# A decay buffer for each half, K's product on GpSimd alone, F's mask as one operation, and one order for all groups of chunks

## The chip, the cores and the metric

The kernel runs on one core of one Trainium2 chip. Its metric is the device time of one execution in microseconds (us), the median of several runs. The engines of the core work side by side, each through its own instructions in order: TensorE (PE, with weight loads as PEld), VectorE (DVE), ScalarE (ACT), GpSimd (POOL) and SyncE (SP), whose queue issues nearly all the DMAs. They wait for each other through semaphores.

## The reference, cut to what matters

A recurrence over 768 steps for 4 x 8 heads of dimension 40, and behind it a mixture of four attention experts.

```python
for t in range(768):                     # state is 40 x 40 for each batch and head
    y[t]  = r[t] @ state
    Sa    = state @ a[t]
    state = state * w[t][None, :] - outer(Sa, b[t]) + outer(v[t], k[t])
x = y, heads side by side                # (4, 768, 320)
...
for e in range(4):                       # causal attention, head dimension 64
    out += gate[e] * softmax(mask(x wq[e] (x wk[e])^T / 8)) (x wv[e]) wo[e]   # two experts of four per row
```

All is float32. The change lies in the recurrence alone.

## The kernel before, in words

**Chunks and groups.** The 768 steps are cut into `NC = 24` chunks of 32, and the chunks into `NW = 6` groups W of four. Within a chunk the recurrence is turned into products of matrices of 32 x 32 and 32 x 40, for all 32 heads. Sixteen heads lie in each half of the partitions (index s or t), and a group's heads and chunks are prepared in two halves, `a = 0` and `1`.

**Preparing a group.** `prep(W, a)` makes the operands of one half. Its pieces have one letter each, and "0" or "1" ahead of it in the schedules is the half:

- `w`, `e`: loads of the decays (EW) and of a (EA); `l`, `u`: loads of the keys' two partition halves (EK, into KB). Each goes through SP's queue.
- `a` (L179): a scan over the decays into SUF, their products to the chunk's end. `b` (L181, L182): a copy and a reciprocal for the next scan. `s` (L184): the scan into SC, their products from the chunk's start.
- `f`, `g` (L176): two range flags on ScalarE, which read EW and write into GB.
- `x` or `X` (L188): AB = EA * SC, two operations, on VectorE or GpSimd.
- `k`, `p`, `K`, `H` (L192): KB = KB * SUF, in place; `K` and `H` are the b part and the k part on GpSimd, two operations each, `p` is the b part on VectorE, `k` both parts on VectorE.

EW's second half lies in an area of KB for the first group, and all later groups use one buffer for both halves, so `1w` waits for the scans and flags of half 0.

**The inversion.** `m0` and `m1` (`mm`) make 64 products each (L208), masked into GB (L210) and transposed into GK (L211), which GpSimd masks twice (L213). `L` (L222) copies GB into MT, `t` with a number runs that many of the 28 steps (L230, L232) of a triangular inversion on VectorE, `T` (L234, L235) transposes the result, `B` and `D` (L241) spread it on ScalarE, and `P` and `Q` (L248, 128 products each) complete it; `Q` ends with an addition on VectorE (L255).

**A chunk.** `chunk(c)` has steps `v` (L293), `g` (L297, L299), `u` (L302, L304), `w` (L307, L308), `f` (L311 and the mask L314), `t` (L319, L320), `y` (L323, L325), `z` (L327 and the output's DMA), `q` (L334) and `s` (L343 and the state's update L350). `keys` (L279, L280) transposes the next chunk's keys. The mask is two operations on VectorE of 64 partitions by 512: `FX[q, t]` gets the half t of PF times a triangular mask; the blocks of FX off that half stay at the zeros that `fill` wrote.

**The order.** The loop over n runs the steps in the order of `MAIN`, ten slots (0 to 9) for each n, in which `f`, `t`, `y` and `z` belong to chunk n - 1, `v` to n + 1 and the rest to n. `SIDE` says what of the next group's preparation follows each slot: key r is the chunk relative to 4 (W - 1), and "/" goes to the next slot. `LOADS` adds the loads of the chunks' own operands. Each engine takes its instructions in this order. `START` prepares group 0, `AHEAD` loads and partly prepares group 1 before the loop, and `SIDE1` is an order of its own for the rest of group 1.

Of the kernel before, what the change touches and what calls it, by code (L numbers as in the profile page):

```python
# [7 lines left out]
F32 = mybir.dt.float32  # L8
AF = mybir.ActivationFunctionType
OP = mybir.AluOpType  # L10
# [11 lines left out]
NW, NC = 6, 24  # L22

SIDE = {
    -3: "/0w///0e",
    -2: "//////0l//0f0g/0a0b0s",
    -1: "1w0u0X0K0H/1a1b///1l/1e///1f1g1s1u1X",
    0: "1p1H///m0//////m1L",
    1: "/t14//B/////t14",
    2: "/T////////P",  # L30
    3: "///D//////Q",
}
START = "x0 0w 0l0u 0e 1w 1l1u 1e x1 c0 0a 0b 0f 0g 0k 0s 0x 1a 1b 1f 1g m0 1k 1s 1x x2 m1 L B k0 t28 T D"
AHEAD = "0w 0l0u 1l1u 0e 0a 0b 0f 0g 0s 0K 0H 0X 1w 1e"

SIDE1 = {
    0: "1a1b1K1H/1f1g/1s1X/m0",
    1: "////m1L/t4//t14",
    2: "/t10T//B",
    3: "///P///D///Q",  # L40
}


def layouts(r, k, v, w, a, b):
# [18 lines left out]

def constants():
    f = np.float32
    cm = np.zeros((128, 261), f)
    cm[:, :128] = np.eye(128)
    j = np.arange(128)
    cm[:, 128:160] = j[:, None] % 32 < np.arange(32)[None, :]
    cm[:, 160:192] = -(np.arange(32)[None, :] < j[:, None] % 32).astype(f)  # L70
    cm[:, 192] = -1.25
    cm[:, 193] = 0.8
    cm[:, 195] = j // 32 % 2 == 0
    cm[:, 196] = j // 32 % 2
    cm[:, 197:229] = cm[:, 128:160] * cm[:, 195:196]
    cm[:, 229:261] = cm[:, 128:160] * cm[:, 196:197]
    return {"CM": cm}


def recurrence(tc, ctx, I, xT, FL, CM, early, tail=None):  # L80
    nc = tc.nc
    ep = early.enter_context(tc.tile_pool(name="early", bufs=1, side="right"))
    sp = ctx.enter_context(tc.tile_pool(name="rec", bufs=1))
    pp = ctx.enter_context(tc.tile_pool(name="rps", bufs=1, space=PSUM))
    V, A, T, PL, SY = nc.vector, nc.scalar, nc.tensor, nc.gpsimd, nc.sync
# [7 lines left out]
    def ring(name, shape, n, pool=sp, dt=F32):  # L93
        return [pool.tile(shape, dt, name=f"{name}{i}") for i in range(n)]

    A.dma_start(CM, I["CM"])
    ident, mask, maskn, mask2 = CM[:, 0:128], CM[:, 128:160], CM[:, 160:192], (CM[:, 197:229], CM[:, 229:261])
    d1 = ep.tile([104, 1056], BF, name="D1")
    EW0 = ring("EW", [104, 1056], 1, ep)[0]
    SUFr = ring("SUF", [104, 1057], 2, ep)  # L100
    D1P = ring("D1P", [104, 1056], 1, ep)[0]
    MT = ring("MT", [128, 1056], 1, ep)[0]
# [22 lines left out]
    GT = ring("GT", [128, 8, 2, 40], 1)[0]  # L125
    XT = ring("XT", [104, 16, 64], 1)[0]
    EAr = EAr, GKr[1].rearrange("p n r t -> p (n r t)")[0:104, 0:1024].rearrange("p (n t) -> p n t", t=32)
    EWr = EW0, KBr[1].rearrange("p x c t n -> p (x c t n)")[0:104, 0:1056]

    D0 = SC128[2].rearrange("p n t -> p (n t)")[:, 0:2048].rearrange("p (n r t) -> p n r t", n=32, r=2)  # L130
    two = (0, 1)
# [4 lines left out]
    def fill(x):  # L136
        if x == 0:
            for t in EWr:
                V.memset(t[32:64], 1.0)
            PL.memset(KBr[0][32:64], 0.0)  # L140
            PL.memset(ABr[0], 0.0)
            V.memset(d1, 0.0)
            V.memset(d1[:, ::132], 1.0)
            for t in SUFr:
                V.memset(t[:, 1056:1057], 1.0)
            V.memset(FL, 0.0)
            V.memset(D1P, 0.0)
        elif x == 1:
            PL.memset(MT, 0.0)
            PL.memset(RB, 0.0)  # L150
            PL.memset(RX, 0.0)
            PL.memset(FX, 0.0)
            PL.memset(SD, 0.0)
            PL.memset(R2, 0.0)
        else:
            V.memset(PS[32:64], 0.0)
            V.memset(PF[32:64], 0.0)
            PL.memset(D0, 0.0)
            PL.memset(BD, 0.0)
            PL.memset(ABr[1], 0.0)  # L160
            PL.memset(KBr[1][32:64], 0.0)
# [3 lines left out]
    def prep(w, a):  # L165

        half = slice(32 * a, 32 * a + 32)
        EW, SUF, sc, ab, kb = EWr[a if w == 0 else 0], SUFr[a], SC[w % 3][:, half], ABr[w % 2][:, half], KBr[w % 2][:, 4 * a:4 * a + 4]
        pc, ea = PC[w % 3][:, 8 * a:8 * a + 8], EAr[a if w == 0 else 0]
        sv = SUF[:, 1:1057].rearrange("p (n c) -> p n c", c=33)  # L170
        def load(t, src, which=two):
            for s in which:
                SY.dma_start(t[rows(s)], I[src][w, a, s])
        def flag(x):
            i = 2 * w + a
            A.activation(GB[0:104].rearrange("p (h n) c -> p h n c", n=4), EW.rearrange("p (h n c) -> p h n c", n=4, c=33)[:, :, :, 1:33], AF.Relu, bias=CM[0:104, 192 + x:193 + x],  # L176
                         scale=1.0 - 2.0 * x, accum_out=FL[0:104, 2 * i + x:2 * i + x + 1])
        def suf():
            V.tensor_tensor_scan(SUF[:, 0:1056][:, ::-1], EW[:, ::-1], d1[:, ::-1], 1.0, op0=OP.mult, op1=OP.add)  # L179
        def per():  # L180
            V.tensor_copy(pc, sv[:, ::4, 0])  # L181
            V.reciprocal(D1P[:, ::132], pc)  # L182
        def pre():
            V.tensor_tensor_scan(flat(sc), EW, D1P, 0.0, op0=OP.mult, op1=OP.add)  # L184
        def amul(e):
            for s in two:
                x = ab[rows(s), :, 32 * s:32 * s + 32]
                e.tensor_tensor(x, ea[rows(s)], sc[rows(s), :, 0:32], op=OP.mult)  # L188
        def kmul(e, k):
            for t in two:  # L190
                x = kb[0:104, :, :, t, 32 * k:32 * k + 32]
                e.tensor_tensor(x, x, sv[:, :, 1:33].rearrange("p (x t c) n -> p x t c n", t=2, c=4)[:, :, t], op=OP.mult)  # L192
        return dict(w=lambda: load(EW, "EW"), e=lambda: load(flat(ea), "EA"),
                    l=lambda: load(kb.rearrange("p x c t n -> p (x c t n)"), "EK", (0,)),
                    u=lambda: load(kb.rearrange("p x c t n -> p (x c t n)"), "EK", (1,)),
                    f=lambda: flag(0), g=lambda: flag(1), a=suf, b=per, s=pre, x=lambda: amul(V), X=lambda: amul(PL),
                    k=lambda: (kmul(V, 0), kmul(V, 1)), p=lambda: kmul(V, 0), K=lambda: kmul(PL, 0), H=lambda: kmul(PL, 1))
# [84 lines left out]
    def chunk(c):  # L282
# [26 lines left out]
        def s_f():  # L309
            for x, t in heads:  # L310
                T.matmul(PF[rows(t, 64), 64 * x:64 * x + 64], VR[:, t, x], RB[:, :, x, t], start=True, stop=True)  # L311
            for t in two:
                q = rows(t, 64)
                V.tensor_tensor(FX[q, t], pf[q], mask[q, None, None, :].to_broadcast([64, 8, 2, 32]), op=OP.mult)  # L314
        def s_t():
            if c == 0:
                return
# [41 lines left out]
    def at(n, s, *fs):  # L359
        jobs.setdefault((n, s), []).extend(fs)  # L360

    def items(W, line, inv, td):

        fs, i = [], 0
        line = line.replace(" ", "")
        while i < len(line):
            x = line[i]
            if x in "LTPQBD":
                fs.append(inv[x])
                i += 1  # L370
            elif x == "t":
                j = i + 1
                while j < len(line) and line[j].isdigit():
                    j += 1
                m = int(line[i + 1:j])
                fs += td[:m]
                del td[:m]
                i = j
            else:
                y = line[i + 1]  # L380
                if x == "x":
                    fs.append(lambda y=y: fill(int(y)))
                elif x == "c":
                    fs += [lambda k=k, y=y: load_c(int(y), k) for k in (range(4) if y == '0' else (1,))]
                elif x == "m":
                    fs.append(lambda y=y: mm(W, int(y)))
                elif x == "k":
                    fs.append(lambda y=y: keys(int(y)))
                else:
                    fs.append(preps[W, int(x)][y])  # L390
                i += 2
        return fs

    preps = {(w, a): prep(w, a) for w in range(NW) for a in range(2)}
    for W in range(1, NW):
        inv = invert(W)
        td = list(inv["t"])
        for r, line in (SIDE if W > 1 else SIDE1).items():
            for k, part in enumerate(line.split("/")):
                n = 4 * (W - 1) + r  # L400
                assert k < 10
                at(max(n, 0), k if n >= 0 else 0, *items(W, part, inv, td))
        assert not td

    LOADS = {"v": lambda n: (n + 2, 0), "w": lambda n: (n + 1, 1), "y": lambda n: (n, 2), "f": lambda n: (n, 3)}
# [2 lines left out]
    for f in items(0, START, inv, list(inv["t"])):  # L408
        f()
    units[0]["v"]()  # L410
    for f in items(1, AHEAD, None, None) + items(0, "PQ", inv, None):
        f()
    load_c(1, 0)
    for n in range(NC + 1):
# [396 lines left out]
def body(tc, I, out):  # L811
    with ExitStack() as ctx:
# [24 lines left out]


_INS = {"EW": (6, 2, 2, 40, 1056), "EA": (6, 2, 2, 40, 1024), "EK": (6, 2, 2, 40, 2048), "V1": (24, 128, 320), "VX": (24, 2, 32, 640), "RB": (24, 2, 40, 512),
        "RX": (24, 2, 40, 512), "CM": (128, 261),  # L840
        "WQK": (128, 1536), "WVG": (128, 780), "WO": (128, 640), "MM": (128, 256), "RAW": (32, 768, 6, 40)}


# [18 lines left out]
```

## Time and profile before

| | before |
|---|---|
| median of 3 runs | 648.43 us (646.29 to 649.72) |
| the profiled execution | 647.44 us |
| its span, first to last instruction | 645.6 us |
| TensorE products, weight loads | 555.9 us (86%), 504.7 us (78%) |
| VectorE | 488.5 us (76%) |
| ScalarE | 347.3 us (54%) |
| GpSimd | 256.0 us (40%) |
| mean granted TensorE clock | 0.973 |
| L192 on GpSimd (KB) | 32 operations, 45.6 us |
| L188 on GpSimd (AB) | 20 operations, 44.5 us |
| L314 on VectorE (F's mask) | 48 operations, 32.8 us |

The recurrence takes the span up to about 385 us, the mixture the rest. A share of busy time is a mean over stages with different limits. In the chain that ended last each piece is the work that the next one waited for, so it says which engine set the time where. "issue" there is time in which an engine waited for nothing that the profile shows.

### The profile page before, as it was taken

The numbers are of one execution on the slowest core, as the hardware profiler recorded it, in microseconds if no ns is written. First come the engines' busy times: TensorE is split into PE (matmuls) and PEld (weight loads), VectorE is DVE, ScalarE is ACT, GpSimd is POOL, SyncE is SP. The second block draws the span as 40 slices with busy tenths as digits, with TensorE's granted clock in tenths as the row PEclk, the third lists the DMA queues.
The fourth block names the chain that finished last, engine by engine and source line by source line (L and its number), as shares of the span: only waits on it lengthen the run. The fifth ranks groups of instructions, "written<-read, shape, count | busy, mean of one in ns | idle before, by whom it ended". The sixth has DMA issues, their size and how long they took to land.

```text
span 645.6 us, 23340 instructions
## 1 busy us (share of the span) xinstructions
PE 555.9 (86%) x9961; PEld 504.7 (78%) x9961; DVE 488.5 (76%) x987; ACT 347.3 (54%) x726; POOL 256.0 (40%) x238
## 2 busy tenths in 40 slices
PE   0247689899899989989999987998999899999995
PEld 0237678889798988989899977887798787987784
DVE  7986487869769786886823346999998998798792
ACT  3015244545535634553544633775877686777883
POOL 7546812720651471075000023265353356234550
PEclk9999798999999999998999997998999999999998
DMA  5231124434523633452133625321312031110101
GB/s 169 64 103 35 54 82 126 105 91 120 153 67 96 154 80 116 107 151 66 49 88 81 188 58 128 97 50 57 87 46 78 6 86 58 55 27 23 62 2 67
DMA packets 42256, 53.82 MB, mean 83 GB/s; under 512 B 19808, under 2 KB 33376, under 8 KB 41184
## 3 DMA queue, kind: packets, MB, share of 16 engines
q1 hardware_dynamic: 42000, 52.12, 29.3%
q8 instruction: 80, 1.31, 0.9%
q14 instruction: 32, 0.26, 0.1%
q10 hardware_dynamic: 144, 0.13, 0.1%
HBM read 38.08 MB, written 7.86 MB: 71 GB/s over the span
## 4 chain that ended last, share of the span: by engine, by line
PE 54%; DVE 28%; issue 6%; ACT 4%; DMA 4%; SPq 0%; DVEq 0%; ACTq 0%
PE pk L248 6%; PE pt L619 5%; PE ot L744 4%; PE pf L323 4%; PE ps L343 3%; PE pk L208 3%; PE sc L699 3%; PE pt L755 3%; PE pf L325 3%; PE pt L729 3%; DVE TP L230 3%; DVE MT L232 3%; PE pg L293 3%; DVE m L709 3%; PE pk L279 3%
## 5 line engine op out<-in xcount | busy, mean ns | idle before, releaser
L721 POOL TENSOR_TENSOR P<-P,m 128x128 f32<-128x128 f32 (+2 forms) x96 | 89.1, 950 | 116.6 <-DVE m L717 61.4
L188 POOL TENSOR_TENSOR AB<-EA,SC 40x1024 f32<-40x1024 f32 x20 | 44.5, 2224 | 93.9 <-DVE SC L184 74.2
L710 ACT ACTIVATE P<-sc,m 128x128 f32<-128x128 f32 (+2 forms) x96 | 60.8, 634 | 26.0 <-DVE m L709 15.1
L744 PE MATMUL ot<-pt,vv 128*128 128x256 f32 (+1 forms) x384 | 61.1, 291 | 5.9 <-DVE ots L750 5.4
L699 PE MATMUL sc<-ks,qs 128*128 128x384 f32 (+4 forms) x256 | 62.7, 347 | 2.8 <-ACT P L710 1.9
L733 DVE TENSOR_TENSOR pt<-pt,pt 128x384 fp32r<-128x384 f32 (+1 forms) x96 | 59.0, 619 | 5.3 <-ACT pt L732 3.6
L709 DVE TENSOR_REDUCE m<-sc 128x1 f32<-128x128 f32 (+2 forms) x96 | 58.8, 616 | 1.1 <-PE sc L702 0.5
L744 PEld LDWEIGHTS ot<-pt,vv 128*128 128x128 f32 x384 | 51.3, 190 | 10.2 <-DVE ots L750 8.1
L732 ACT ACTIVATE pt<-pt 128x384 fp32r<-128x384 f32 (+1 forms) x96 | 52.0, 543 | 10.5 <-PE pt L729 9.0
L729 PE MATMUL pt<-CM,P 128*128 128x128 f32 x336 | 52.9, 275 | 3.9 <-DVE qs L628 2.6
L323 PE MATMUL pf<-FX,LS 128*40 128x64 f32 x768 | 47.7, 224 | 9.0 <-DVE FX L314 8.8
L192 POOL TENSOR_TENSOR KB<-KB,SUF 104x512 f32<-104x512 f32 x32 | 45.6, 1451 | 23.7 <-DVE SUF L179 12.4
L208 PE MATMUL pk<-KB,AB 104*64 104x64 f32 x768 | 29.6, 246 | 28.5 <-DVE AB L188 28.2
L323 PEld LDWEIGHTS pf<-FX,LS 128*40 128x40 f32 x768 | 42.3, 118 | 12.4 <-DVE FX L314 11.4
L314 DVE TENSOR_TENSOR FX<-pf,CM 64x512 f32<-64x512 f32 x48 | 32.8, 684 | 24.4 <-PE pf L311 24.0
L208 PEld LDWEIGHTS pk<-KB,AB 104*64 104x64 f32 x768 | 27.9, 159 | 29.6 <-issue 18.0
L619 PE MATMUL pt<-xh,wq 128*128 128x384 f32 x192 | 42.9, 359 | 4.4 <-DVE qs L628 4.2
L325 PE MATMUL pf<-RX,SD 80*40 80x64 f32 x736 | 45.9, 222 | 0.0
L699 PEld LDWEIGHTS sc<-ks,qs 128*128 128x128 f32 x256 | 40.7, 192 | 6.5 <-ACT P L710 5.9
L213 POOL TENSOR_TENSOR GK<-GK,CM 128x512 f32<-128x512 f32 x24 | 27.1, 1128 | 46.6 <-DVE GK L211 45.5
L299 ACT ACTIVATE GT<-pg,CM 128x320 f32<-128x320 f32 x48 | 22.7, 523 | 40.2 <-PE pg L297 40.2
L304 ACT ACTIVATE R<-pu 32x640 f32<-32x640 f32 x48 | 33.3, 693 | 19.4 <-PE pu L302 18.9
(147 smaller groups left out, 1388.1 us busy)
## 6 DMA issues: line engine op xcount, KB each, us to landing
KB<-in_EK SPq DMA_DIRECT2D x24, 320.0 KB
ks<-ks SPq DMA_DIRECT2D x32, 192.0 KB
V<-in_V SPq DMA_DIRECT2D x24, 160.0 KB
R<-in_VX SPq DMA_DIRECT2D x48, 80.0 KB
RX<-in_RX SPq DMA_DIRECT2D x48, 80.0 KB
RB<-in_RB SPq DMA_DIRECT2D x48, 80.0 KB
xT<-XT SPq DMA_DIRECT2D x24, 160.0 KB
out_dram<-o SPq DMA_DIRECT2D x24, 160.0 KB
```

The lines of the kernel that those rows point to most:

```text
L208: T.matmul(PK[rows(t, 64), x // 2, y:y + 64], ab[:, n], kb[0:104, 4 * a + x, c, t], start=True, stop=True)
L323: T.matmul(pf[rows(r), x], ls[:, x, r], FX[:, :, x, r], start=True, stop=c == 0)
L325: T.matmul(pf[rows(r), x], SD[:, x, r], RX[:, :, x, r], start=False, stop=True)
L619: T.matmul(p, w, x, start=(j == 0), stop=(j == len(prs) - 1))
L699: T.matmul(ps[:, c, 0:cw], QS[b][:, e, o], KS[b][:, e, z, k], start=(z == 0), stop=(z == 1 and not last), skip_group_check=True)
L709: V.tensor_reduce(m[:, 0, t:t + 1], ps[:, 0:ch, 0:cw], axis=AX.XY, op=OP.max, negate=True)
L710: later(DE, lambda: A.activation(pv, ps[:, 0:ch, 0:cw], AF.Exp, bias=m[:, 0, t:t + 1], accum_out=m[:, 1, t:t + 1]))
L721: PL.tensor_tensor(P[:, 0:n], P[:, 0:n], m[:, 3, t:t + 1].to_broadcast([128, n]), op=OP.mult)
L729: T.transpose(p[:, 128 * y:128 * y + 128], st["P"][t][:, 128 * c:128 * c + 128], ident)
L732: A.activation(h, p[:, 0:n], AF.Copy)
L733: later(DL, lambda: V.tensor_tensor(l, p[:, 0:n], f32(h), op=OP.subtract))
L744: T.matmul(po[:, 128:256] if one else po, VV[b][:, k, e].rearrange("p a b -> p (a b)"), PT[:, 256 * k:256 * k + (128 if one else 256)], st ...
```

## The change

- **EW has two buffers**, one for each half, in every group. The first group's second half no longer lies in KB.
- **K's product** of half 1 runs on GpSimd (`1K1H`), where half 0's did already; `p` is no longer used. It moves from slot 0 of the group's first chunk to slot 4 of the chunk before.
- **Loads** move: `0w` from slot 1 of r = -3 to slot 4 of r = -4, `1w` from slot 0 of r = -1 to slot 1 of r = -3, `0u` from slot 0 of r = -1 to slot 9 of r = -2, `1l` from slot 4 to slot 1, `1u` from slot 9 to slot 4 and `1e` from slot 5 to slot 6 of r = -1.
- **F's mask** is one operation over 128 partitions by 1024: PF is read twice along a broadcast axis and multiplied by a mask MK that is zero off the half. FX need not be cleared; MK comes with a second small load at the start.
- **Group 1** uses `SIDE` like the others. What `SIDE` puts before the loop stands in `AHEAD`, which now has both halves' scans and products, except `1f1g1s1X`, which follow slot 0 of the first chunk. `m1` and `L` of group 1 move from slot 4 of n = 1 to slot 9 of n = 0, and `P` from slot 3 of n = 3 to slot 9 of n = 2.
- The inversion's 28 steps are split 16 and 12 instead of 14 and 14.

```diff
--- before.py
+++ after.py
@@ -22,23 +22,18 @@
 NW, NC = 6, 24
 
 SIDE = {
-    -3: "/0w///0e",
-    -2: "//////0l//0f0g/0a0b0s",
-    -1: "1w0u0X0K0H/1a1b///1l/1e///1f1g1s1u1X",
-    0: "1p1H///m0//////m1L",
-    1: "/t14//B/////t14",
+    -4: "////0w",
+    -3: "/1w///0e",
+    -2: "//////0l//0f0g/0u0a0b0s",
+    -1: "0X0K0H/1l1a1b///1u1K1H//1e//1f1g1s1X",
+    0: "///m0//////m1L",
+    1: "/t16//B/////t12",
     2: "/T////////P",
     3: "///D//////Q",
 }
 START = "x0 0w 0l0u 0e 1w 1l1u 1e x1 c0 0a 0b 0f 0g 0k 0s 0x 1a 1b 1f 1g m0 1k 1s 1x x2 m1 L B k0 t28 T D"
-AHEAD = "0w 0l0u 1l1u 0e 0a 0b 0f 0g 0s 0K 0H 0X 1w 1e"
-
-SIDE1 = {
-    0: "1a1b1K1H/1f1g/1s1X/m0",
-    1: "////m1L/t4//t14",
-    2: "/t10T//B",
-    3: "///P///D///Q",
-}
+
+AHEAD = "0w1w 0l0u 1l1u 0e 0f0g 0a0b0s 0X0K0H 1a1b 1e 1K1H", "1f1g1s1X"
 
 
 def layouts(r, k, v, w, a, b):
@@ -63,7 +58,7 @@
 
 def constants():
     f = np.float32
-    cm = np.zeros((128, 261), f)
+    cm = np.zeros((128, 325), f)
     cm[:, :128] = np.eye(128)
     j = np.arange(128)
     cm[:, 128:160] = j[:, None] % 32 < np.arange(32)[None, :]
@@ -73,6 +68,8 @@
     cm[:, 195] = j // 32 % 2 == 0
     cm[:, 196] = j // 32 % 2
     cm[:, 197:229] = cm[:, 128:160] * cm[:, 195:196]
+    for t in range(2):
+        cm[:, 261 + 32 * t:293 + 32 * t] = cm[:, 128:160] * (j // 64 == t)[:, None]
     cm[:, 229:261] = cm[:, 128:160] * cm[:, 196:197]
     return {"CM": cm}
 
@@ -93,10 +90,12 @@
     def ring(name, shape, n, pool=sp, dt=F32):
         return [pool.tile(shape, dt, name=f"{name}{i}") for i in range(n)]
 
-    A.dma_start(CM, I["CM"])
+    MK = sp.tile([128, 64], F32, name="MK")
+    A.dma_start(CM, I["CM"][:, 0:261])
+    A.dma_start(MK, I["CM"][:, 261:325])
     ident, mask, maskn, mask2 = CM[:, 0:128], CM[:, 128:160], CM[:, 160:192], (CM[:, 197:229], CM[:, 229:261])
     d1 = ep.tile([104, 1056], BF, name="D1")
-    EW0 = ring("EW", [104, 1056], 1, ep)[0]
+    EWr = ring("EW", [104, 1056], 2, ep)
     SUFr = ring("SUF", [104, 1057], 2, ep)
     D1P = ring("D1P", [104, 1056], 1, ep)[0]
     MT = ring("MT", [128, 1056], 1, ep)[0]
@@ -125,7 +124,6 @@
     GT = ring("GT", [128, 8, 2, 40], 1)[0]
     XT = ring("XT", [104, 16, 64], 1)[0]
     EAr = EAr, GKr[1].rearrange("p n r t -> p (n r t)")[0:104, 0:1024].rearrange("p (n t) -> p n t", t=32)
-    EWr = EW0, KBr[1].rearrange("p x c t n -> p (x c t n)")[0:104, 0:1056]
 
     D0 = SC128[2].rearrange("p n t -> p (n t)")[:, 0:2048].rearrange("p (n r t) -> p n r t", n=32, r=2)
     two = (0, 1)
@@ -149,7 +147,6 @@
             PL.memset(MT, 0.0)
             PL.memset(RB, 0.0)
             PL.memset(RX, 0.0)
-            PL.memset(FX, 0.0)
             PL.memset(SD, 0.0)
             PL.memset(R2, 0.0)
         else:
@@ -165,7 +162,7 @@
     def prep(w, a):
 
         half = slice(32 * a, 32 * a + 32)
-        EW, SUF, sc, ab, kb = EWr[a if w == 0 else 0], SUFr[a], SC[w % 3][:, half], ABr[w % 2][:, half], KBr[w % 2][:, 4 * a:4 * a + 4]
+        EW, SUF, sc, ab, kb = EWr[a], SUFr[a], SC[w % 3][:, half], ABr[w % 2][:, half], KBr[w % 2][:, 4 * a:4 * a + 4]
         pc, ea = PC[w % 3][:, 8 * a:8 * a + 8], EAr[a if w == 0 else 0]
         sv = SUF[:, 1:1057].rearrange("p (n c) -> p n c", c=33)
         def load(t, src, which=two):
@@ -309,9 +306,8 @@
         def s_f():
             for x, t in heads:
                 T.matmul(PF[rows(t, 64), 64 * x:64 * x + 64], VR[:, t, x], RB[:, :, x, t], start=True, stop=True)
-            for t in two:
-                q = rows(t, 64)
-                V.tensor_tensor(FX[q, t], pf[q], mask[q, None, None, :].to_broadcast([64, 8, 2, 32]), op=OP.mult)
+            V.tensor_tensor(FX.rearrange("q t x s n -> q t (x s) n"), PF.rearrange("q (x n) -> q x n", n=32)[:, None].to_broadcast([128, 2, 16, 32]),
+                            MK.rearrange("q (t n) -> q t n", t=2)[:, :, None, :].to_broadcast([128, 2, 16, 32]), op=OP.mult)
         def s_t():
             if c == 0:
                 return
@@ -392,14 +388,15 @@
         return fs
 
     preps = {(w, a): prep(w, a) for w in range(NW) for a in range(2)}
+    at(0, 0, *items(1, AHEAD[1], None, None))
     for W in range(1, NW):
         inv = invert(W)
         td = list(inv["t"])
-        for r, line in (SIDE if W > 1 else SIDE1).items():
-            for k, part in enumerate(line.split("/")):
-                n = 4 * (W - 1) + r
+        for r, line in SIDE.items():
+            n = 4 * (W - 1) + r
+            for k, part in enumerate(line.split("/") if n >= 0 else ""):
                 assert k < 10
-                at(max(n, 0), k if n >= 0 else 0, *items(W, part, inv, td))
+                at(n, k, *items(W, part, inv, td))
         assert not td
 
     LOADS = {"v": lambda n: (n + 2, 0), "w": lambda n: (n + 1, 1), "y": lambda n: (n, 2), "f": lambda n: (n, 3)}
@@ -408,7 +405,7 @@
     for f in items(0, START, inv, list(inv["t"])):
         f()
     units[0]["v"]()
-    for f in items(1, AHEAD, None, None) + items(0, "PQ", inv, None):
+    for f in items(1, AHEAD[0], None, None) + items(0, "PQ", inv, None):
         f()
     load_c(1, 0)
     for n in range(NC + 1):
@@ -837,7 +834,7 @@
 
 
 _INS = {"EW": (6, 2, 2, 40, 1056), "EA": (6, 2, 2, 40, 1024), "EK": (6, 2, 2, 40, 2048), "V1": (24, 128, 320), "VX": (24, 2, 32, 640), "RB": (24, 2, 40, 512),
-        "RX": (24, 2, 40, 512), "CM": (128, 261),
+        "RX": (24, 2, 40, 512), "CM": (128, 325),
         "WQK": (128, 1536), "WVG": (128, 780), "WO": (128, 640), "MM": (128, 256), "RAW": (32, 768, 6, 40)}
```

## The prediction

> **What bounds the kernel now.** I read the page first (busy shares, the chain that ended last), then the windows by stage, then who waited for whom on TensorE, then the timeline around the long waits.
>
> ```profile
> PE 555.9 (86%) x9961; PEld 504.7 (78%) x9961; DVE 488.5 (76%) x987; ACT 347.3 (54%) x726; POOL 256.0 (40%) x238
> PE 54%; DVE 28%; issue 6%; ACT 4%; DMA 4%; SPq 0%; DVEq 0%; ACTq 0%
> ```
>
> TensorE carries most of the chain, VectorE a quarter. The change touches only the recurrence (0 to about 385 us); the mixture behind it is left alone. So I cut the recurrence at the starts of the key transposes (L279), one per chunk. Columns: window, its length, then busy us of each engine, granted clock, DMA share, GB/s.
>
> ```profile
> core 0: us, PE busy (x) PEld busy (x) DVE busy (x) ACT busy (x) POOL busy (x), PEclk, DMA share, GB/s
> 70.20:84.30 14.10, 12.42 (x281) 11.29 (x281) 3.59 (x6) 4.05 (x6) 8.49 (x6) 0.82 0.30 90
> 84.30:95.70 11.40, 9.98 (x256) 9.06 (x256) 10.57 (x31) 6.09 (x9) 2.55 (x4) 1.00 0.20 54
> 95.70:112.20 16.50, 15.27 (x387) 14.24 (x385) 12.81 (x14) 7.64 (x12) 4.32 (x2) 0.90 0.49 123
> 112.20:131.20 19.00, 17.25 (x451) 16.18 (x448) 15.13 (x15) 8.27 (x13) 13.80 (x10) 0.91 0.38 91
> 167.70:185.90 18.20, 15.80 (x449) 14.76 (x448) 15.73 (x15) 7.99 (x13) 12.85 (x9) 1.00 0.37 100
> 185.90:222.40 36.50, 35.28 (x964) 32.78 (x961) 27.68 (x50) 19.02 (x29) 8.86 (x8) 1.00 0.45 119
> 222.40:240.90 18.50, 16.40 (x451) 15.43 (x449) 15.78 (x15) 8.01 (x13) 13.95 (x10) 0.95 0.38 95
> 278.10:296.90 18.80, 16.99 (x451) 16.16 (x448) 15.24 (x15) 8.04 (x13) 13.08 (x9) 0.91 0.37 96
> 333.40:346.90 13.50, 13.50 (x387) 12.73 (x385) 4.41 (x6) 5.71 (x9) 0.00 (x0) 1.00 0.17 52
> 346.90:366.50 19.60, 19.60 (x516) 18.03 (x513) 5.78 (x8) 9.89 (x15) 0.00 (x0) 1.00 0.62 185
> ```
>
> The last two rows are the floor. A bare chunk is pure TensorE at 9.8 us (19.6 / 2). One with 128 inversion products (L248) is 13.5. An `mm` half adds 2.1 (L208, below). The stage at the head of a group holds one chunk, a set of L248 and an `mm` half: floor 15.6. It took 19.0, 18.2, 18.5 and 18.8. That is the largest loss, 12.1 us over four groups. The remaining three chunks (36.5, quoted once) have a floor of 9.8 + 9.8 + 13.5 + 2.1 = 35.2. The first group's three chunks took 14.1 + 11.4 + 16.5 = 42.0. Late chunks have nothing to win.
>
> ```profile
> PE pf L323 <- DVE FX L314: 8.8, 11, 2.1
> PE ps L319 <- issue: 1.8, 1, 1.8
> PE pu L302 <- issue: 1.7, 1, 1.7
> PE pk L248 <- issue: 1.7, 1, 1.7
> ```
>
> Those are TensorE's waits between 60 and 390 us. The three "issue" waits fall into the head stages of groups W=2, 3 and 5 (at 123, 175 and 288 us), and the longest L323 wait into that of W=4, so each head stage has one stop. In W=4 it is this:
>
> ```profile
> 232.89 3.85 DVE L192 TENSOR_TENSOR KB<-KB,SUF 104x512 f32<-104x512 f32 x2 [1.03 <-DMA KB<-in_EK]
> 233.91 2.08 PE L208 MATMUL pk<-KB,AB 104*64 104x64 f32 x64
> 236.66 1.38 DVE L314 TENSOR_TENSOR FX<-pf,CM 64x512 f32<-64x512 f32 x2
> 238.09 0.36 PE L323 MATMUL pf<-FX,LS 128*40 128x64 f32 x3 [2.10 <-DVE FX L314]
> ```
>
> VectorE waits for the second K load in `1p`, with the mask behind it, and TensorE waits for the mask.
>
> The three "issue" stops I read as TensorE's own instructions arriving late. The DMA queues ahead of the stop in W=5 (279.6 to 286.4 us), and at the same place of W=4 (224.3 to 231.3), in columns packets, MB and share of 16 engines:
>
> ```profile
> q1 hardware_dynamic: 380, 1.23, 71.1%
> ```
> ```profile
> q1 hardware_dynamic: 358, 1.21, 69.3%
> q8 instruction: 2, 0.03, 1.8%
> ```
>
> Same load on the data queue, but no instruction packet ahead of the stop and two where there was no stop. That is an inference from one pair. In W=2 the mask was late as well:
>
> ```profile
> 125.61 2.89 PE L208 MATMUL pk<-KB,AB 104*64 104x64 f32 x64
> 127.13 1.38 DVE L314 TENSOR_TENSOR FX<-pf,CM 64x512 f32<-64x512 f32 x2
> ```
>
> Without the 1.7 us stop TensorE would have been through with L208 at some 126.0, and the mask ended at 128.5. So there, and as I take it in W=3 and W=5, one of the two waits hides the other: removing the late mask alone gains almost nothing. After a stop the products are slower too: 64 of L208 took 2.89 here, 2.08 in W=4's row.
>
> **The change part by part.**
>
> *K on GpSimd alone, loads earlier.* Per group (W=2 to 5) two VectorE operations (3.85 us with their waits) leave the head stage, and GpSimd gets two more, 1.2 us each (median, next fence). SP issues the same loads, the last K load five slots earlier and its E load after it, with `0u` and `1w` out of the crowded chunk into the ones before. None waits for a reader there: every buffer it fills was read last at least a slot earlier. The mask then stands directly behind the inversion's add and is ready before TensorE asks. In W=4 that takes 18.5 to the floor plus 0.4 (the three-chunk stages stand 1.3 over theirs, some 0.4 a chunk), 16.0: **-2.5**. In the other three the gain is (19.0 + 18.2 + 18.8) / 3 - 16.0 = 2.7 each if the stop goes, near 0 if it stays. Of the large loads issued in the chunk ahead, an EW pair and one of three EK leave, about a third of the bytes, so I take one stop of three as gone: **-2.7** (bounds 0 and -8.1).
>
> GpSimd's queue in that chunk becomes 0X, 0K, 0H, 1K, 1H, 1X, then GK's masks. Its end, 1X, feeds the second `mm` half, one chunk later. Now, in W=3:
>
> ```profile
> 181.81 2.67 POOL L192 TENSOR_TENSOR KB<-KB,SUF 104x512 f32<-104x512 f32 x2
> 189.65 2.08 PE L208 MATMUL pk<-KB,AB 104*64 104x64 f32 x64
> ```
>
> GpSimd is done at 184.5 and the half starts at 189.7, so some 5 us cover the reordering.
>
> *F's mask in one operation.* Price of one by the nearest row of 1024 elements, half of 2.47:
>
> ```profile
> 15.25 2.47 DVE L188 TENSOR_TENSOR AB<-EA,SC 40x1024 f32<-40x1024 f32 x2
> ```
>
> So 1.23 instead of 1.38: 0.15 saved per chunk. Bounds: 1.38 (no gain) and 0.69, if one operation costs what one of the two costs now. It reaches the end only where TensorE waits for the mask: two chunks in each of four groups, 8 x 0.15 = **-1.2**. The dropped clear of FX and the second constant load lie in idle time at the start.
>
> *t16/t12 instead of t14/t14.* 28 steps between the same masks; state add and output come two steps later, some 0.5 us, while TensorE is busy with `v`. I take 0; if `v` did not cover it, +0.5 in each of five groups.
>
> *First group in the others' order, EW in two buffers.* Here everything is priced by these rows:
>
> ```profile
> 12.81 2.35 DVE L184 TENSOR_TENSOR_SCAN SC<-EW,D1P 104x1056 f32<-104x1056 f32 x1
> 52.16 6.66 POOL L192 TENSOR_TENSOR KB<-KB,SUF 104x512 f32<-104x512 f32 x4 [12.42 <-DVE SUF L179]
> 58.78 4.41 POOL L188 TENSOR_TENSOR AB<-EA,SC 40x1024 f32<-40x1024 f32 x2
> 61.50 3.91 DVE L179 TENSOR_TENSOR_SCAN SUF<-EW,D 104x1056 f32<-104x1056 f32 x1
> 63.25 2.09 PE L208 MATMUL pk<-KB,AB 104*64 104x64 f32 x64 [0.23 <-POOL AB L188]
> 68.85 0.66 DVE L210 TENSOR_TENSOR GB<-pk,CM 128x512 f32<-128x512 f32 x1
> 70.19 1.65 PE L279 MATMUL pk<-CM,KB 104*128 104x104 f32 x8 [4.85 <-DVE GK L211]
> 84.15 2.00 DVE L222 STREAM_TRANSPOSE MT<-GB 128x1024 f32<-128x1024 f32 x1
> 84.28 0.93 PE L279 MATMUL pk<-CM,KB 104*128 104x104 f32 x8 [1.49 <-DVE GK L211]
> 198.47 0.93 PE L279 MATMUL pk<-CM,KB 104*128 104x104 f32 x8
> ```
> ```profile
> L192 POOL TENSOR_TENSOR KB<-KB,SUF x32: 1170/1195/3235, 52.2 to 293.5; 104x512 f32<-104x512 f32 x32
> ```
>
> The scan at 61.50 took 3.91: it waited for GpSimd's product to end (58.78 + 4.41 = 63.19), then ran 2.36. So a scan and a GpSimd product take turns. The Trainium skill's "GPSIMD Engine Reference", section "Key points", says that GpSimd shares its SBUF interfaces with VectorE and contends with instructions that have two SBUF inputs. The trace agrees (3.91 against 2.35); the rule speaks against moving work to GpSimd, and the first rival below prices it.
>
> The new order starts 0X only behind `0s` (52.5 + 2.4 = 54.9), and 0K, 0H behind 0X. With scans `1a` and `1s` taking turns: 54.9 + 4.4 + 4 x 1.2 + 2 x 2.36 + 0.4 for the copies = 69.2 before `m0` can start; now 63.25. `m0`, cold, takes 2.1 to 3.7 (I take 3.3), mask and transpose 1.4: first L279 at 73.9, now 70.19, **+3.7**. The four TensorE steps up to `m1`, some 0.4 of a bare chunk or 3.9, reach it at 77.8; it waits for 1X, 69.2 + 4 x 1.2 + 4.4 = 78.4, and ends at 80.5. VectorE's mask, transpose (together 1.3) and MT (2.0) and F's mask (1.2) end at 85.0, then some 0.9 of L323: second L279 at 85.9, now 84.28, +1.6. From there the group runs like W=3, where 198.47 to 222.4 is 23.9: fourth L279 at 109.8, now 112.2: **-2.4** over all. The time is regained since `m1` no longer stands just ahead of L279 (1.49 there) and the inversion starts a chunk earlier. Bounds: 36.5 less the L325 and state transposes that chunk 0 lacks (an estimate: 0.9 each, like 8 L279) is 34.7 against 42.0, so -7.3; and +3.7 if nothing is regained.
>
> **Sum:** -2.5 - 2.7 - 1.2 - 2.4 = -8.8 us. The profiled execution (647.44 us; its span of 645.6 and 1.8 around it) goes to 638.6; against the median of 648.43, which lies 1.0 higher, 639.6.
>
> **The rivals.**
>
> *GpSimd becomes the wait (slower).* One queue now holds both K halves and 1X. If its products ran at 6.66 / 4 = 1.67 with VectorE taking turns, and the late K load still held 1K, 1X would end 4 x 0.5 + 2.4 later plus the load's delay. It decides when 1X ends after the time `mm` needs it, 189.7 in W=3 (187 with the stage shortened). At 4 us beyond that, each of four groups loses 4 - 2.7 = 1.3, and the first group adds 4 to its -2.4: 5.2 + 1.6 - 1.2 = +5.6, 654.0. For it: 69.2 and 78.4 above are already on the path. Against: 5 us of cover, and GpSimd busy only 13 of 18 us in the head stages.
>
> *The stops stay.* Then the mask's lateness was covered in three groups: -2.5 - 1.2 - 2.4 = -6.1, 642.3; with a new stop in W=4 and no net gain at the start, -1.2: 647.2, no change that can be told. For it: the count of instructions and of large loads is the same, only their spacing changes. The Trainium skill's "Runtime: NRT & Kernel Launch", section "Instruction fetch mechanics", says that fetching is mostly hidden behind slower dispatch. By that rule the three stops are something else and stay, which is this rival's time; the missing q8 row speaks against the rule, but only once.
>
> *All stops go:* -8.8 - 5.4 = -14.2, 634.2.
>
> **How the numbers follow.** Forecast (one stop of three goes, give or take 3 us at the start) 0.45; stops stay but the rest works, 0.15; all go, 0.12; stops stay and the start gives nothing, 0.17; GpSimd becomes the wait, 0.11. About 0.5% (3.2 us) is what a measurement of this kernel can tell from no change. The first three and little of the others end below 645.2: faster 0.71, same 0.17, slower 0.12. Range 633 to 648.5: from "all go" to the no-change case, leaving out the slower rival and a little at the bottom.
>
> **What would show it.** Right: no VectorE L192 after 40 us; L314 24 times at about 1.2; head stages at 16 to 16.5 unless they hold an "issue" wait; first L279 near 74, the fourth near 110. Wrong: L208 waiting for GpSimd in the groups from W=2 on; "issue" waits still in three or four head stages or moved to the chunk before; a scan held by GpSimd pushing the inversion's add past TensorE; or the mask at 1.4 or more.

## The result and the profile after

The changed kernel takes 632.7 us (median; 631.9 to 633.6) against 648.7 for the one before: ratio 0.976, interval 0.973 to 0.979. That is 7 us under the forecast of 639.6, a little under the low end of the range, and near the time of the rival "all stops go" (634.2). Measured again beside the kernel before, the same kernel stood at 0.978 (0.971 to 0.984) and 0.971 (0.967 to 0.974) of it. Executions over 1.5% above the fastest of their kernel are left out of the ratios, and the profiled ones of e1 and e2 are of that kind, so I read from them where a stop lies and not what the whole takes. In the changed kernel and those made from it the lines have other numbers: L276 for L279, L205 for L208, L208 for L211, L245 for L248, L309 for the mask (L314), L319 for L323, L189 for KB, L185 for AB, L181 for the scan into SC (L184), L299 for L302 and L315 for L319. In e2, e3 and e8, made from the kernel before, they are those of before. One slip in the text above: `1u` stood at slot 8 of the chunk before the group's first, not 9, so it moves four slots.

From the page of the changed kernel, busy shares, chain and two groups of instructions:

```profile
PE 550.8 (87%) x9961; PEld 500.5 (79%) x9961; DVE 476.1 (75%) x955; ACT 347.4 (55%) x726; POOL 276.8 (44%) x245
PE 60%; DVE 20%; issue 5%; ACT 4%; POOL 4%; DMA 4%; SPq 0%; DVEq 0%; ACTq 0%; POOLq 0%
L189 POOL TENSOR_TENSOR KB<-KB,SUF 104x512 f32<-104x512 f32 x40 | 66.3, 1690 | 0.6 <-DMA KB<-in_EK 0.2
L309 DVE TENSOR_TENSOR FX<-pf,MK 128x1024 f32<-128x1024 f32 x24 | 29.1, 1213 | 23.7 <-PE pf L308 23.7
```

VectorE's part of the chain falls from 28% to 20%; the shares of busy time hardly move. The stages, cut at the same places (columns as above):

```profile
73.50:86.80 13.30, 12.00 (x281) 11.00 (x281) 6.08 (x11) 4.79 (x8) 8.38 (x8) 0.84 0.20 58
86.80:97.80 11.00, 10.00 (x259) 9.07 (x257) 10.28 (x28) 5.35 (x8) 0.00 (x0) 1.00 0.35 101
97.80:111.30 13.50, 13.50 (x386) 12.73 (x385) 10.94 (x9) 8.19 (x13) 5.04 (x3) 1.00 0.54 150
111.30:126.90 15.60, 15.39 (x449) 14.63 (x448) 12.72 (x12) 8.00 (x13) 15.53 (x10) 1.00 0.34 88
162.80:179.40 16.60, 15.66 (x452) 14.75 (x449) 11.91 (x12) 8.03 (x13) 16.52 (x10) 1.00 0.29 84
179.40:215.20 35.80, 35.19 (x961) 32.72 (x960) 27.96 (x47) 18.99 (x29) 10.76 (x10) 1.00 0.48 132
215.20:230.60 15.40, 15.40 (x451) 14.62 (x448) 11.79 (x12) 8.05 (x13) 15.34 (x9) 1.00 0.33 90
266.50:281.90 15.40, 15.40 (x451) 14.63 (x449) 11.76 (x12) 8.01 (x13) 15.14 (x10) 1.00 0.33 89
```

Two head stages (W=4 and 5) are TensorE from end to end: 15.4 busy of 15.4. TensorE's waits between 60 and 390 us that answer to those above:

```profile
PE pk L205 <- POOL KB L189: 5.1, 2, 4.5
PE pf L319 <- DVE FX L309: 4.0, 6, 1.2
PE pk L245 <- issue: 0.9, 1, 0.9
```

One "issue" stop is left of three (0.9 us, W=3; a fourth one before, 0.7 us at L307, lay in the same stage and is gone too), and a wait for GpSimd is new, at the start. Where the 15.7 us of the recurrence went, by the starts of L276 against those of L279 (exact to 0.01):

| stretch | before | after | difference |
|---|---|---|---|
| start to the first key transposes | 70.19 | 73.47 | +3.3 |
| first to fourth (group 1) | 42.00 | 37.80 | -4.2 |
| the four head stages | 74.58 | 63.00 | -11.6 |
| all later chunks | 179.7 | 176.5 | -3.2 |
| up to the last key transposes | 366.48 | 350.82 | -15.7 |

Of the 3.2 us of the later chunks, 0.8 are one chunk of W=4 that before took 13.3 us at a granted clock of 0.93, where its like in the other groups took 12.5 to 12.6. What follows the last key transposes took 1.4 us more (645.6 - 366.5 = 279.1, now 631.3 - 350.8 = 280.5). Of these, 1.3 lie in the last stage of the recurrence, where the granted clock was 0.91 in this execution and 1.00 before.

### The profile page after: what moved, and what is told of

Read it like the earlier page. It is cut to its first block, busy times and chain, and to the rows that moved or that the text cites. A ratio compares the mean times of both kernels' runs of the same rounds, so it can differ in the third digit from the quotient of the medians.

```text
span 631.3 us, 23310 instructions
## 1 busy us (share of the span) xinstructions
PE 550.8 (87%) x9961; PEld 500.5 (79%) x9961; DVE 476.1 (75%) x955; ACT 347.4 (55%) x726; POOL 276.8 (44%) x245
## 3 DMA queue, kind: packets, MB, share of 16 engines
q8 instruction: 80, 1.31, 0.9%
## 4 chain that ended last, share of the span: by engine, by line
PE 60%; DVE 20%; issue 5%; ACT 4%; POOL 4%; DMA 4%; SPq 0%; DVEq 0%; ACTq 0%; POOLq 0%
PE pk L245 5%; PE pt L616 5%; PE ps L339 4%; PE ot L741 4%; PE pk L205 4%; PE pf L319 4%; PE sc L696 4%; PE pf L321 3%; PE pt L726 3%; PE pt L752 3%; PE pg L290 3%; PE pk L276 3%; DVE m L706 3%; PE pu L299 3%; PE pg L294 3%
## 5 line engine op out<-in xcount | busy, mean ns | idle before, releaser
L185 POOL TENSOR_TENSOR AB<-EA,SC 40x1024 f32<-40x1024 f32 x20 | 45.5, 2275 | 99.0 <-DVE SC L181 98.2
L189 POOL TENSOR_TENSOR KB<-KB,SUF 104x512 f32<-104x512 f32 x40 | 66.3, 1690 | 0.6 <-DMA KB<-in_EK 0.2
L205 PE MATMUL pk<-KB,AB 104*64 104x64 f32 x768 | 30.3, 247 | 33.7 <-DVE AB L185 28.5
L205 PEld LDWEIGHTS pk<-KB,AB 104*64 104x64 f32 x768 | 28.3, 160 | 34.9 <-issue 18.1
L319 PE MATMUL pf<-FX,LS 128*40 128x64 f32 x768 | 47.6, 224 | 4.3 <-DVE FX L309 4.0
L319 PEld LDWEIGHTS pf<-FX,LS 128*40 128x40 f32 x768 | 42.1, 118 | 7.5 <-DVE FX L309 6.4
L309 DVE TENSOR_TENSOR FX<-pf,MK 128x1024 f32<-128x1024 f32 x24 | 29.1, 1213 | 23.7 <-PE pf L308 23.7
L296 ACT ACTIVATE GT<-pg,CM 128x320 f32<-128x320 f32 x48 | 22.7, 523 | 42.2 <-PE pg L294 42.2
L726 PEld LDWEIGHTS pt<-CM,P 128*128 128x128 f32 x336 | 36.7, 141 | 7.4 <-issue 3.2
```

Source lines behind the costliest of these rows:

```text
L205: T.matmul(PK[rows(t, 64), x // 2, y:y + 64], ab[:, n], kb[0:104, 4 * a + x, c, t], start=True, stop=True)
L319: T.matmul(pf[rows(r), x], ls[:, x, r], FX[:, :, x, r], start=True, stop=c == 0)
L726: T.transpose(p[:, 128 * y:128 * y + 128], st["P"][t][:, 128 * c:128 * c + 128], ident)
```

## The experiments

They ask two things: what emptied the head stages, and what the start costs. Ratios are to the kernel before on the same chip. The kernel before spread from 643 to 657 us, the changed one over 1.7, 5.6 and 1.3 us on its three occasions, so single stages of a profile are often the sharper reading.

**e1: the mask alone.** Before, with MK and the single mask operation of the diff.

> The kernel before with F's mask as one operation and nothing else. Both theories: one operation at 1.21 us for two at 1.37 together, so 0.15 us where TensorE waits for the mask, at most 2 or 3 chunks of a group: 0.6 to 2 us less than before, head stages of the groups still at 18 to 19 us. If the mask alone were worth more (0.4 us in each of the chunks at the second and third place of a group, as the changed kernel has it), 3 us less.

Measured 0.998 (0.994 to 1.002): no difference that can be told. In its trace the second and third chunk of a group take 12.37 and 10.13 us (before 12.53 and 10.40), -0.43 a group. The head stages stay at 18.5 to 22.7.

**e2: K on GpSimd alone.**

```diff
-    0: "1p1H///m0//////m1L",
+    0: "1K1H///m0//////m1L",
```

> The kernel before with K's b part of half 1 on GpSimd instead of VectorE, at the same place in the order, loads as before. Theory 'crowd' (TensorE's instructions come late behind the crowd of loads): the 'issue' stops stay in three of the four head stages, which stay at 18 to 19 us; only the W=4 stage falls, to about 16: 2.5 us less in all. Theory 'mask' (VectorE's late mask is the loss and the stops only lie beside it): all four head stages fall to about 16: 10 to 12 us less.

Measured 0.992 (0.987 to 0.996). Head stages of W=2 to 5, and from TensorE's waits between 100 and 300 us those for the mask and the long stops:

```profile
111.10:128.00 16.90, 15.69 (x452) 14.74 (x449) 12.65 (x13) 8.27 (x13) 12.21 (x9) 1.00 0.45 110
164.40:188.20 23.80, 20.49 (x452) 19.10 (x449) 12.29 (x13) 8.05 (x13) 14.46 (x11) 0.78 0.29 76
224.60:240.00 15.40, 15.40 (x451) 14.63 (x448) 12.27 (x13) 8.05 (x13) 11.10 (x8) 1.00 0.43 115
276.50:297.40 20.90, 18.06 (x450) 17.08 (x449) 11.99 (x13) 7.98 (x13) 14.49 (x11) 0.84 0.35 87
```
```profile
PE pf L323 <- DVE FX L314: 3.6, 6, 0.7
PE pk L248 <- issue: 3.1, 1, 3.1
PE ps L319 <- issue: 2.8, 1, 2.8
PE pu L302 <- issue: 1.2, 1, 1.2
```

No long wait for the mask is left (0.7 at most), and W=4, which had only that, is at the floor. The three stops stay, in the same three stages and at the same lines. So far theory "crowd" has it right, though the three stages are at 16.9 to 23.8 us and not at 18 to 19, and the whole gained 5.4 us where it allowed 2.5.

**e3: the loads alone.** Before, with two EW buffers and the new slots of `w`, `u`, `l`, `e`; `1p1H` in its old place.

> The kernel before with two EW buffers and the new slots of the loads, K's product on VectorE in its old place, the mask as two operations, group 1 in its old order. Theory 'crowd': no 'issue' stop is left in the head stages, and K's load is there in time, so VectorE's product runs straight after the inversion's scan: head stages 16 to 16.5, 9 to 11 us less than before. Theory 'mask': the product still holds VectorE for 3.3 us in front of the mask, taking turns with GpSimd, and the head stages stay at 17.5 or more: 2 to 4 us less.

Measured 0.999 (0.995 to 1.003). The same views:

```profile
113.30:129.10 15.80, 15.73 (x453) 14.81 (x448) 12.09 (x12) 8.27 (x13) 11.53 (x8) 1.00 0.34 88
165.60:187.60 22.00, 18.87 (x451) 17.63 (x448) 15.63 (x15) 8.03 (x13) 14.21 (x9) 0.84 0.24 63
224.10:241.80 17.70, 15.63 (x449) 14.73 (x448) 16.76 (x15) 8.01 (x13) 14.49 (x9) 1.00 0.31 81
278.20:296.10 17.90, 15.83 (x453) 14.83 (x449) 16.92 (x15) 8.08 (x13) 14.69 (x9) 1.00 0.28 77
```
```profile
PE pf L323 <- DVE FX L314: 7.7, 8, 2.1
PE pk L248 <- issue: 2.8, 1, 2.8
```

Two of three stops are gone, but now the mask is late by some 2 us in W=4 and W=5, where VectorE's product still stands in front of it. Its load is there, but taking turns with GpSimd its two operations took 4.95 and 4.99 us in these stages; in W=2 they took 3.70, and the mask was in time. Neither theory gives both the stops and the times: there are two losses, and in W=5 e2 and e3 together show that each covers the other.

**e8: both, and nothing else of the change.** e3 with `1u1K1H` at slot 4 and no `1p1H`, so that K's product also starts earlier, as in the changed kernel.

> The kernel before with the loads' new slots, two EW buffers and K's product of half 1 on GpSimd at its new place, and nothing else: mask as two operations, 14 and 14 steps, group 1 in its old order. If the two waits hid each other, this pair gives what neither gives alone: head stages at 15.4 to 16, 9 to 12 us less than before, ratio 0.981 to 0.986. If parts simply add (0.9916 and 0.9992 alone), ratio 0.991.

Measured 0.979 (0.972 to 0.986). Alone the parts gave -0.8% and -0.1%, together -2.1%; -0.9%, the sum of the two, lies outside the interval. The changed kernel stands at 0.978 on the same chip, so these two parts are nearly all of the change. Its head stages (that W=3 has no stop in this execution may be chance, as the next runs show):

```profile
112.20:127.60 15.40, 15.40 (x452) 14.62 (x448) 10.88 (x12) 8.28 (x13) 15.25 (x11) 1.00 0.34 91
164.10:179.50 15.40, 15.40 (x452) 14.63 (x449) 12.03 (x13) 8.03 (x13) 14.89 (x9) 1.00 0.30 92
215.90:231.60 15.70, 15.50 (x453) 14.66 (x449) 12.93 (x13) 8.08 (x13) 15.62 (x10) 1.00 0.30 89
268.00:283.80 15.80, 15.61 (x454) 14.66 (x449) 12.07 (x13) 8.09 (x13) 15.04 (x10) 1.00 0.34 88
```

**e0 and e5: the changed kernel again, and the crowd put back.** e0 has no edit; this is e5's.

```diff
-    -3: "/1w///0e",
-    -2: "//////0l//0f0g/0u0a0b0s",
-    -1: "0X0K0H/1l1a1b///1u1K1H//1e//1f1g1s1X",
+    -3: "////0e",
+    -2: "//////0l//0f0g/0a0b0s",
+    -1: "1w0u0X0K0H/1l1a1b///1u1K1H//1e//1f1g1s1X",
```

> The changed kernel once more, so that the others here stand beside it on the same chip: 0.976 of before.

> The changed kernel with two of its loads put back into the crowd: 1w and 0u at slot 0 of the chunk before a group's first, as before. All else as changed. Theory 'crowd': the fetches of TensorE's instructions slip again behind the loads, 'issue' stops of 1.2 to 3 us come back in two or three of the four head stages, which go from 15.4 to 17 to 22 us: 5 to 12 us more than the changed kernel, and a wider spread of its runs. Theory 'VectorE' (with its product gone, VectorE no longer holds anything up, and the loads are no matter): within 1 us of the changed kernel, head stages at 15.4 to 16.5.

Measured 0.978 (0.971 to 0.984) for e0 and 0.974 (0.968 to 0.979) for e5: no loss. In e5's profile W=2, 4 and 5 stay at 16.0, 15.4 and 15.4. So theory "crowd", as I had put it, falls: the bytes that I counted as the third that leaves are not what stops TensorE. Both have a long stop in W=3 in the profiled execution (2.8 and 3.3 us). e0's, with the stages around it and the queues ahead of it (161.4 to 168.2 us):

```profile
170.78 2.37 PE L245 MATMUL pk<-MT,BD 64*64 64x64 f32 x44 [2.79 <-issue]
```
```profile
161.30:170.90 9.60, 6.66 (x179) 6.03 (x178) 8.68 (x8) 5.02 (x8) 9.60 (x5) 1.00 0.47 121
170.90:181.20 10.30, 10.30 (x161) 9.63 (x162) 1.91 (x2) 2.23 (x4) 7.89 (x6) 0.51 0.06 19
```
```profile
q1 hardware_dynamic: 344, 0.95, 54.4%
```

and those of e8, which had no stop there, at the same place (164.3 to 171.1 us):

```profile
q1 hardware_dynamic: 476, 1.15, 55.3%
q8 instruction: 1, 0.02, 0.9%
```

Again no instruction packet ahead of the stop, and one where there is none. The missing packet of e0 came just behind that window, at 168.25 us, when TensorE had stood for 0.3 us (168.2 to 169.5 us):

```profile
q1 hardware_dynamic: 128, 0.17, 51.6%
q8 instruction: 1, 0.02, 5.8%
```

It landed at 169.46, and TensorE went on at 170.78. The traces settle what two pairs could not: all 28 "issue" stops of TensorE between 100 and 300 us in the fourteen traces end 1.2 to 1.7 us after a packet of the instruction queue has landed (16 KB each: 80 packets, 1.31 MB before). And the later the packet, the longer the stop. In W=3, where the long stop lies in the products of L245 (L248 before), the packet due there came 3.2 to 3.8 us into the stage in the three traces without that stop (e4, e8, e9), 4.4 to 4.9 us in the four with one of 0.9 to 1.2 us (the changed kernel in its first and third trace, e4 on the second chip, e10), and 6.0 to 8.4 us in the seven others, where it took 1.7 to 3.3 us. So these stops are TensorE waiting for its instructions. What makes a packet late is not shown: in the two windows above the same loads were issued.

The Trainium skill's "Runtime: NRT & Kernel Launch", section "Instruction fetch mechanics", has the fetch mostly hidden; here it is not in this stage, by up to 3.3 us (e5).

**e9: the last three loads back in their old slots.** This kernel also runs `1K1H` of group 1 twice, which changes that group's values and its time up to the fourth L276 (115.1 us).

```diff
-    -1: "0X0K0H/1l1a1b///1u1K1H//1e//1f1g1s1X",
-    0: "///m0//////m1L",
+    -1: "0X0K0H/1a1b///1l/1e///1f1g1s1u1X",
+    0: "1K1H///m0//////m1L",
```

> The changed kernel with the last three loads of a group back in their old slots (1l at 4, 1e at 5, 1u at 8) and so 1K1H at slot 0 of the next chunk; 1w and 0u stay early. Theory 'last load': a fetch of TensorE's instructions stops the engine where it falls due in the 5 to 7 us behind the last EK load, whatever the other loads do. Then the stops of W=2 and W=5 come back (in L299 and L315, 1.2 to 2.8 us), those stages go from 15.5 to 17 to 21, and the kernel takes 3 to 8 us more than the changed one. Theory 'chance' (stops come and go with the execution, not with the slots): no more than 1 us more, W=2 and W=5 at 15.4 to 15.7.

Measured 0.983 (0.977 to 0.989); beside it the changed kernel (label e0b):

> The changed kernel, for comparison on the same chip. 0.976 of before; head stages at 15.4 to 15.7 apart from the second one (W=3), which has an 'issue' stop in some executions (15.4 to 23.4).

0.971 (0.967 to 0.974). Between the medians of the runs counted lie 9.4 us; in the profiled executions 5.7 of the difference are there already at the fourth L276 (115.1 against 109.4), behind group 1's second product. In the profiled execution, the fastest of four (635.0 to 647.4), TensorE's stops from 100 to 300 us are

```profile
PE pu L299 <- issue: 1.1, 1, 1.1
PE ps L315 <- issue: 0.3, 1, 0.3
```

These are W=2 and W=5, at the lines of the kernel before, and W=3 has none; but they are small, and the stages are at 16.7 and 15.8, less than I expected. What can be said over all traces: with `1u` at slot 8 (before, e1, e2, e9) W=2 and W=5 both have a stop, 0.3 to 2.8 us; with `1u` at slot 4 (the changed kernel three times, e3, e4 twice, e5, e6, e8, e10) none over 0.4. In W=2 that is four of four with a stop of 1.1 us or more against ten of ten with none; in W=5 the two sets touch (0.3 in e9, 0.4 in e10). `1l` and `1e` move along with `1u` in all of these, so the slots of the last three loads together decide over the stop in W=2 and, less surely, in W=5; which of the three does is not shown. The stop in W=3 is open: its length changed between executions of the very same kernel (16.5 and 23.4 us for that stage in e0b and e0).

**e4: group 1 in its old order.** The changed kernel with `SIDE1` and the old `AHEAD`, run on two chips.

> The changed kernel with group 1's own order and the old list ahead of the loop. First L276 back at about 70.2 (73.5 in the changed kernel), the three chunks after it at 40 to 42 us (37.8). By the two traces the new order is worth 0.9 us at the fourth L276: 633.5. By my forecast of that part, 2.4 us: 635. If the lower clock windows fall elsewhere, up to 2 us either way.

> The changed kernel with group 1's own old order, on the same chip as the changed one. By the traces so far the order itself is worth 0 to 1.4 us at the fourth L276; the rest of its lead was the stop in the W=3 stage, which it did not have: 0 to 5 us less than the changed kernel, more than 2 only if that stop is there again in one and not in the other.

Measured 0.976 (0.970 to 0.982) and 0.973 (0.967 to 0.980, beside 0.971 for the changed kernel). Its fourth L276 stands at 109.9 and 111.1; the changed kernel's at 111.3, 109.8 and 109.4. e1, which has the old order too, reached it at 110.5. The new order of group 1 is worth nothing that these runs can tell.

**e6: GpSimd starts with K.**

```diff
-... 0a0b0s 0X0K0H 1a1b 1e 1K1H"
+... 0a0b0s 0K0H0X 1a1b 1e 1K1H"
```

> The changed kernel with 0K0H ahead of 0X in the list before the loop, so that GpSimd starts at 52.4 us, when SUF is there, and not at 55.3, when SC is. If GpSimd's queue is what holds the first mm half (67.2 to 68.3 us in the changed kernel): that half starts at 63 to 64.5, first L276 at 67.5 to 70 (73.5), fourth at 105 to 108 (111.3): 3 to 6 us less than the changed kernel. If the inversion's end or the clock holds it: less than 1 us.

Measured 0.972 (0.966 to 0.978), beside 0.978 (0.971 to 0.984): not told apart. L205 starts at 67.6, the first L276 at 72.8. GpSimd began 2.9 us earlier, but its first four products then took 8.7 us and AB 6.5 (6.7 and 4.4 in the kernel before), with two scans taking turns among the products and a third during AB. The fourth L276 came at 110.8, not at 105 to 108.

**e10: group 1's start on VectorE.**

```diff
-AHEAD = "... 0a0b0s 0X0K0H 1a1b 1e 1K1H", "1f1g1s1X"
+AHEAD = "... 0a0b0k0s0x 1e", "1f1g1a1b", "1k1s1x"     # the third part behind m0
```

> The changed kernel with group 1 prepared on VectorE instead of GpSimd: 0a0b0k0s0x behind the inversion of group 0, 1a1b behind slot 0 of the first chunk, 1k1s1x behind m0. Where the two engines take turns, the faster one is the better place: VectorE needs 0.6 us for a product of 512 where GpSimd needs 1.2, and 1.2 for one of 1024 where GpSimd needs 2.2. Then the first mm half starts at 63 us (68.3 in the changed kernel), first L276 at 66 to 68 (73.5), the second at 80 to 83 (86.8) and the fourth at 104 to 107 (111.3): 4 to 7 us less than the changed kernel. If VectorE becomes the bound there instead (its products in front of the mask of the first chunk): less than 2 us.

Measured 0.969 (0.965 to 0.973), the lowest ratio, but not told apart from the changed kernel beside it (0.971). From its timeline:

```profile
52.61 2.46 DVE L189 TENSOR_TENSOR KB<-KB,SUF 104x512 f32<-104x512 f32 x4
63.33 2.09 PE L205 MATMUL pk<-KB,AB 104*64 104x64 f32 x64
66.90 0.93 PE L276 MATMUL pk<-CM,KB 104*128 104x104 f32 x8 [1.49 <-DVE GK L208]
75.91 3.66 PE L205 MATMUL pk<-KB,AB 104*64 104x64 f32 x64 [5.21 <-issue]
85.06 0.93 PE L276 MATMUL pk<-CM,KB 104*128 104x104 f32 x8
```

The first L276 came 6.5 us earlier, as expected. The rest was not as expected: the second `mm` half waited 5.2 us (its AB ended at 75.8 on VectorE) and ran at 3.66 instead of 2.1: the second L276 is at 85.1, where the changed kernel on this chip had 84.9, and the fourth at 109.6 against 109.4. The gain turned into a new wait.

## Why the prediction was right, and where its sizes were off

*The lost time is in the head stages, and each has two waits of which one hides the other.* Right in the main. e2 and e3 show it for W=5, and e8 that the two parts give more together than their sum. In W=2 the loads alone removed both waits (15.8 us in e3), W=4 had only the mask, and W=3 kept its stop in e2 and e3, so there it is not shown. The forecast built on it, one stop of three gone and 639.6, did not come; what came is the rival "all stops go", which had 0.12.

*"Issue" as instructions that come late.* Right, and shown by the packets that every stop ends behind. That the number of instructions is the same, as the rival "the stops stay" argued, did not keep the stops.

*W=4 falls to the floor: -2.5.* It fell by 3.1 (18.51 to 15.39). The difference of 0.6 is the 0.4 a chunk that I had left as residue, and a floor of 15.4 instead of 15.6.

*One stop of three goes: -2.7.* This is the term that was mis-sized. W=2, 3 and 5 gave 56.1 to 47.6, -8.5; two stops went and the third shrank to 0.9. I had let the number of stops follow the share of bytes that leave (an EW pair and one EK). e5 put just those back and lost nothing. What matters for W=2, and as it seems for W=5, is when the last three loads are issued, which the prediction named only in passing.

*The mask: 1.23 for 1.38, -1.2 in all.* The price was right (1.213). It reached the end more often than I took: e1 shows -0.43 a group, and the changed kernel -0.58 in W=2 (12.53 + 10.40 to 12.37 + 9.98). The last 0.15 may be the 16 and 12 split, which I had at 0; no run had that alone.

*The start.* Forecast: first L276 at 73.9, second `mm` half at 78.4, second L276 at 85.9, fourth at 109.8. Measured: 73.5, 79.2, 86.8 and 111.3 in the profiled execution, 109.4 and 109.8 in two others. The steps:

```profile
55.29 6.38 POOL L185 TENSOR_TENSOR AB<-EA,SC 40x1024 f32<-40x1024 f32 x2 [15.26 <-DVE SC L181]
61.74 11.10 POOL L189 TENSOR_TENSOR KB<-KB,SUF 104x512 f32<-104x512 f32 x8
68.32 3.68 PE L205 MATMUL pk<-KB,AB 104*64 104x64 f32 x62 [0.66 <-POOL KB L189]
73.47 1.65 PE L276 MATMUL pk<-CM,KB 104*128 104x104 f32 x8 [1.48 <-DVE GK L208]
79.17 2.08 PE L205 MATMUL pk<-KB,AB 104*64 104x64 f32 x64
```

Taking turns is visible in the first row: two products that take 4.4 alone took 6.4, with one scan of 2.3 among them. Here the rule of the shared interfaces in the Trainium skill's "GPSIMD Engine Reference", section "Key points", holds. GpSimd began 3.1 us later, behind the scan into SC (55.29 against 52.16), and from there to the first `mm` half it took 13.0 us against 11.1; the first L276 came 3.3 us later, where the sum had 3.7.

The -2.4 that the sum gives to the new order is not borne out. The fourth L276 stood at 109.4 to 112.2 in four traces with this order (the changed kernel three times, and e5), and at 109.9, 110.5 and 111.1 with the old order and the single mask (e4 twice, e1). That two of them came near 109.8 is luck: the old order got there as well.

*GpSimd becomes the wait.* It did, twice, at the start only (4.5 and 0.7 us); from W=2 on no L205 waits for it, as the 5 us of cover said.

## What to carry to other kernels

Where two waits of different kinds end at nearly the same place, test them together: each alone gave 0.1 to 0.8% here, both 2.1%. Count a stop by the stage it lies in, not by its own length, and give the case that all of them go the chance that one common cause deserves. When a stop has no cause in the profile, look past its end too: the packet that came behind the window told more than the one that was missing in it. Where two engines take turns, work moved from one to the other may gain nothing unless it leaves the path (e6, e10), and a stage filled earlier may only wait later.

## What the runs showed of the hardware that I had not expected

A stop of 2.8 us cost 8.0: in e0 the W=3 stage took 23.4 us against 15.4 in e8. In the 10.3 us behind the stop TensorE was busy without a gap and the granted clock was 0.51 (rows above). The Trainium skill's "TensorE: Matmul & The Clock Gate", section "What's actually happening", has the full clock back after some 3.4 us of sustained work; in e0 it took three times as long, and why is not shown. The stops of 0.9 to 1.2 us in this stage (the changed kernel, e0b, e10, e4 on the second chip) left the clock at 1.00 and the stage 1.2 to 1.4 us longer.

Between 1.2 and 2.8 us the length of the stop alone does not decide. The stop of e6 and its stage:

```profile
170.96 1.46 PE L245 MATMUL pk<-MT,BD 64*64 64x64 f32 x44 [2.37 <-issue]
```
```profile
162.30:180.30 18.00, 15.63 (x452) 14.71 (x449) 11.91 (x12) 8.03 (x13) 17.74 (x11) 1.00 0.29 78
```

The clock stayed, and the stage lost 2.6 us. e1's stop of 2.0 us in the same stage brought the mean clock down to 0.78, and the stage to 22.7 us. In the kernel before, two stops of 1.7 us differ in the same way: the one in W=2 was followed by 3.4 us at a clock of 0.50, the one in W=3 by none.
